# Four more pairs turned on TensorE, four more joined products, two stores at the end and a new order of the work

## The chip, the core and the metric

The kernel runs on one core of a Trainium2 chip. The metric is the device time of one execution in microseconds (us). Five engines work side by side: TensorE (PE in the profile, with its weight loads as PEld), VectorE (DVE), ScalarE (ACT), GpSimd (POOL) and the queue that issues the transfers, SyncE (SP). Each engine runs its own instructions strictly in the order in which the program lists them, and waits for the others by semaphores.

## What is computed

Two stages follow one another. The first is an attention with random features, for 8 batches of 8 heads, 576 positions of 64 numbers and 128 features. The second is a layer with a gate, applied to the 4608 tokens that come out.

```python
def phi(x):
    h = x @ omega.T - sum(x * x) / 2
    return exp(h - max(h)) / sqrt(m)
q_p, k_p = phi(q_s), phi(k_s)
kv, z = k_p^T v, sum(k_p)
out = (q_p @ kv) / (q_p @ z + 1e-06)
x = out, heads side by side: 4608 tokens of 512
h = x @ w_in
g = h * erf(softplus(h))
return g @ w_out
```

## The kernel before, in words

Two heads make a pair, and there are 32 pairs (N, line 32), numbered 0 to 31, four for each batch. For each pair TensorE projects k and q on omega, VectorE takes maxima, and ScalarE the exponentials. That gives the features `fk` and `fq`, 128 positions by 128 features in nine blocks. Then `key_values` (line 1103) sums the product of k's features with v into the bank `kvp` (36 small matmuls), and `attend` (line 1129) multiplies q's features with it into the banks `nd` (36 more; "the last product" in what follows). For `nd` q's features must lie with the features on the partitions, so `fq` has to be turned. This is done in two ways:

- For pairs below ROWS = 20 (line 785), `turn` (line 1118) has TensorE transpose the nine blocks, three into each of three PSUM banks `pt`. A copy for each bank by ScalarE or VectorE brings them into the tile `qh`.
- For pairs 20 to 31, `flip` (line 1080) transposes 32 by 32 blocks in one VectorE instruction. SyncE then stores the whole to DRAM (`dq<-fq`) and fetches it back in four transfers (`qh<-dq`), which put the blocks in their places. For these pairs the exponentials of q are written in another order of the blocks.

BEHIND (line 791) is `range(8, 31)`: for those pairs the product `nd` of a pair n is not a step of its own. It is issued right behind `kvp` of pair n + 1, as one step (`key_values` with `beside`, line 1103). For the other pairs `nd` is a step of its own. The quotients are written to the tile `y`, which serves two pairs and of which there is one (SLOTS, line 79). VectorE transposes it, and SyncE's transfers `xs<-y` bring it to the tokens' tile `xs`.

The second stage takes the tokens in six groups (SUPERS, line 33): two of 2 times 288 tokens, then four of 2 times 432. A group runs four quarters of the inner layer. Each quarter has a first product (banks `h`, `hX`, `hY`, `hZ`), the gate on ScalarE, VectorE and GpSimd, and a second product (banks `o`, `oX`, `oY`, `oZ`), which is added into the output tile `os`. Every number is held as a high and a rest part, so that each product is three matmuls. From the third group on, seven products stand for eight, with sums of blocks that VectorE and GpSimd make (tiles `xc` and `gs`). In the last quarter of a group the output rows leave: `keep` (line 1378) issues one store for both token halves `t` of a row tile, which `gemm2` (line 1413) asks for when the second half is done.

The attention of later batches runs between the products of earlier groups. The order is not written out by hand. `build` lists some 4,660 steps with a duration each, and `Plan.order` (line 154) gives each engine, one step at a time, the ready step with the earliest due time. The due times come from the plan of the second stage, carried backwards through the dependencies. The list `DATES` (line 336) then adds a correction to them, by the number of the step:

```python
        for i, x in DATES:
            ops[i].due += x
```

What comes out is the order of the instructions on every engine, SyncE's queue among them. `emit` writes them in that order, and it is fixed when the kernel runs.

Of the kernel before, what the change touches and what calls it, by code (L numbers as in the profile page):

```python
# [108 lines left out]
class Plan:  # L109
# [44 lines left out]
    def order(self, slots, caps):  # L154
# [59 lines left out]
        while True:  # L214
# [121 lines left out]
DATES = ((0, -155.4), (1, 0.9), (2, -0.7), (4, -446.6), (5, -58.8), (6, -11.2), (7, -171), (8, -17.9),  # L336
# [445 lines left out]
YFLIP = 1.5  # L782
YDMA = 4.0
ISSUE = 0.5
ROWS = 20
BOTH = 12
SUMA = ()
JOIN = 1
# [1128 lines left out]
```

## Time and profile before

| what | value |
|---|---|
| median of three runs | 978.97 us (974.37, 978.97 and 979.22) |
| the profiled execution's own time | 971.93 us |
| its span, first to last instruction | 970.2 us |
| PE busy | 954.5 us of it, 98% |
| DVE busy | 761.5 us, 78% |
| ACT busy | 625.4 us, 64% |
| POOL busy | 583.4 us, 60% |
| moved by DMA | 255.64 MB, 263 GB/s on the mean |

The profile shows one execution. Busy time of an engine counts each instant in which at least one of its instructions runs. Matmuls overlap (a matmul of 432 columns shows some 0.36 us, and the next starts 0.20 us after it), so that the rate is read from starts. Line 1523 is the helper that records all instructions; groups are told apart by their tiles.

### The profile page before, as it was taken

The numbers are of one execution on the slowest core, as the hardware profiler recorded it, in microseconds if no ns is written. First come the engines' busy times: TensorE is split into PE (matmuls) and PEld (weight loads), VectorE is DVE, ScalarE is ACT, GpSimd is POOL, SyncE is SP. The second block draws the span as 40 slices with busy tenths as digits, with TensorE's granted clock in tenths as the row PEclk, the third lists the DMA queues.
The fourth block names the chain that finished last, engine by engine and source line by source line (L and its number), as shares of the span: only waits on it lengthen the run. The fifth ranks groups of instructions, "written<-read, shape, count | busy, mean of one in ns | idle before, by whom it ended". The sixth has DMA issues, their size and how long they took to land.

```text
span 970.2 us, 20988 instructions
## 1 busy us (share of the span) xinstructions
PE 954.5 (98%) x7868; PEld 903.8 (93%) x7868; DVE 761.5 (78%) x1161; ACT 625.4 (64%) x1157; POOL 583.4 (60%) x416
## 2 busy tenths in 40 slices
PE   8999999999999999999998999999999999999998
PEld 8899999999999999999998999888999999999997
DVE  6879788767777977768797879789898699668674
ACT  7869787875866766665476375666747547564650
POOL 3234534947747666748496758388686486548620
PEclk9999999999999999999999999999999999999999
DMA  8667779598897798897898999998998776697651
GB/s 250 213 212 235 236 258 329 206 329 317 309 282 227 254 322 285 257 316 232 272 316 249 385 294 322 288 301 262 292 307 248 249 243 219 215 309 220 222 184 74
DMA packets 116388, 255.64 MB, mean 263 GB/s; under 512 B 14272, under 2 KB 31168, under 8 KB 116288
## 3 DMA queue, kind: packets, MB, share of 16 engines
q1 hardware_dynamic: 116128, 254.24, 79.9%
q8 instruction: 63, 1.03, 0.4%
q14 instruction: 37, 0.30, 0.1%
q10 hardware_dynamic: 160, 0.07, 0.0%
HBM read 194.74 MB, written 50.07 MB: 252 GB/s over the span
## 4 chain that ended last, share of the span: by engine, by line
PE 56%; DMA 4%; DVE 4%; SPq 0%; ACT 0%; issue 0%; DVEq 0%; ACTq 0%
PE hX L1523 13%; PE oX L1523 11%; PE hY L1523 7%; PE o L1523 7%; PE oY L1523 5%; PE hZ L1523 4%; PE oZ L1523 3%; DMA wb<-wdc 2%; PE kvp L1523 2%; PE nd L1523 1%; PE p0k L1523 1%; PE p1k L1523 1%; DMA y<-xN 1%; DMA xs<-y 1%; DMA wb<-wdw 1%; DVE os L1523 1%
## 5 line engine op out<-in xcount | busy, mean ns | idle before, releaser
L1523 POOL TENSOR_TENSOR hs<-gs,hs 128x864 f32<-128x864 f32 (+1 forms) x56 | 111.2, 2012 | 112.0 <-ACT gs L1523 82.8
L1523 PE MATMUL o<-gh,w 128*128 128x288 f32 (+1 forms) x704 | 167.4, 317 | 0.0
L1523 PE MATMUL hX<-xh,wb 128*128 128x432 f32 x512 | 161.6, 361 | 1.8 <-DVE y L1523 1.4
L1523 PEld LDWEIGHTS o<-gh,w 128*128 128x128 f32 x704 | 120.8, 188 | 2.1
L1523 PE MATMUL h<-xh,w 128*128 128x288 f32 x512 | 110.6, 300 | 0.0
L1523 PE MATMUL o<-gl,w 128*128 128x288 f32 (+1 forms) x352 | 110.0, 312 | 0.0
L1523 PEld LDWEIGHTS hX<-xh,wb 128*128 128x128 f32 x512 | 96.1, 188 | 7.9 <-issue 1.8
L1523 ACT ACTIVATE hs<-hX 128x432 f32<-128x432 f32 x65 | 34.7, 533 | 104.0 <-PE hX L1523 103.2
L1523 PE MATMUL oX<-th,wb 128*128 128x432 f32 x312 | 97.4, 360 | 2.2 <-DVE os L1523 2.2
L1523 PE MATMUL hX<-xl,wb 128*128 128x432 f32 x256 | 91.8, 359 | 0.0
L1523 ACT ACT_TABLE_LOAD x67 | 86.0, 1283 | 2.1 <-PEq L1908 0.7
L1523 PE MATMUL hY<-xh,wb 128*128 128x432 f32 x256 | 84.0, 363 | 1.2 <-ACT fk L1523 0.4
L1523 PEld LDWEIGHTS h<-xh,w 128*128 128x128 f32 x512 | 84.2, 188 | 0.9 <-ACT fk L1523 0.2
L1523 PE MATMUL h<-xl,w 128*128 128x288 f32 x256 | 75.4, 295 | 0.0
L1523 DVE TENSOR_TENSOR os<-oX,os 128x432 f32<-128x432 f32 x86 | 50.9, 600 | 24.5 <-PE oX L1523 24.3
L1523 ACT ACTIVATE gs<-hs 128x1728 f32<-128x1728 f32 (+1 forms) x48 | 69.4, 1483 | 0.4
L1523 ACT ACTIVATE gs<-gs 128x1728 f32<-128x1728 f32 (+1 forms) x48 | 69.1, 1480 | 0.3
L1523 PEld LDWEIGHTS o<-gl,w 128*128 128x128 f32 x352 | 66.3, 188 | 0.9
L1523 PEld LDWEIGHTS oX<-th,wb 128*128 128x128 f32 x312 | 58.6, 188 | 5.9 <-DVE os L1523 2.9
L1523 POOL TENSOR_TENSOR bl<-hs,bh 128x864 fp32r<-128x864 f32 x22 | 57.5, 2634 | 0.0
L1523 PE MATMUL oX<-tl,wb 128*128 128x432 f32 x156 | 55.9, 359 | 0.0
L1523 POOL TENSOR_TENSOR tl<-gs,th 128x864 fp32r<-128x864 f32 x20 | 44.5, 2246 | 18.8 <-ACT th L1523 13.9
(162 smaller groups left out, 2699.9 us busy)
## 6 DMA issues: line engine op xcount, KB each, us to landing
wb<-wdc SPq DMA_DIRECT2D x232, 256.0 KB, 4.6
wb<-wdw SPq DMA_DIRECT2D x174, 256.0 KB, 4.8
w<-wdw SPq DMA_DIRECT2D x44, 512.0 KB, 6.1
st<-w SPq DMA_DIRECT2D x32, 512.0 KB, 5.7
wdw<-w SPq DMA_DIRECT2D x32, 512.0 KB, 4.7
wdc<-c SPq DMA_DIRECT2D x32, 512.0 KB, 5.9
x<-xR SPq DMA_DIRECT2D x20, 576.0 KB, 6.5
y<-xN SPq DMA_DIRECT2D x20, 576.0 KB, 6.3
```

Source lines behind the costliest of these rows:

```text
L1523: return tc.keep_in_program_order(method(*args, **kwargs))
```

## The change

Four things are changed together:

- ROWS goes from 20 to 24: pairs 20 to 23 take `turn` in place of `flip`, and their q keeps the plain layout and the plain order of the exponentials.
- BEHIND goes from `range(8, 31)` to `range(4, 31)`: `nd` of pairs 4 to 7 is issued behind `kvp` of pairs 5 to 8.
- In the last group `keep` is called for each token half: eight stores of one half in place of four of both.
- DATES is another list, with 2,281 corrections where there were 2,992, so that the whole order of the steps is new.

```diff
-DATES = ((0, -155.4), (1, 0.9), (2, -0.7), (4, -446.6), (5, -58.8), (6, -11.2), (7, -171), (8, -17.9),
...
+DATES = ((0, -150.3), (4, -232.6), (5, 4.5), (6, -14.6), (7, -138.9), (13, -28.1), (14, 2.5),
...
-ROWS = 20
+ROWS = 24
...
-BEHIND = range(8, 31)
+BEHIND = range(4, 31)
...
-    def keep(b, et, o):
-        pl.op("ostore", [("S", 0.1, 1e9)], lambda e: E.o_store(o, b, et), reads=[(o, 0), (o, 1)],
-              plan=clock[0] + 3.0, size=P * 2 * SUPERS[b][0] * 4)
+    def keep(b, et, o, ts=(0, 1)):
+        pl.op("ostore", [("S", 0.1, 1e9)], lambda e: E.o_store(o, b, et, ts), reads=[(o, t) for t in ts],
+              plan=clock[0] + 3.0, size=P * len(ts) * SUPERS[b][0] * 4)
...
                 out(t)
-                if q == NQ - 1 and t:
+                if q == NQ - 1 and b == len(SUPERS) - 1:
+                    keep(b, et, o, (t,))
+                elif q == NQ - 1 and t:
                     keep(b, et, o)
...
-        def o_store(self, o, b, et):
-            sp.dma_start(out[et][:, FROM[b]:FROM[b + 1]], o.ap.rearrange("p t c -> p (t c)"))
+        def o_store(self, o, b, et, ts):
+            T = SUPERS[b][0]
+            at, n = FROM[b] + ts[0] * T, len(ts) * T
+            sp.dma_start(out[et][:, at:at + n], o.ap[:, ts[0]:ts[-1] + 1].rearrange("p t c -> p (t c)"))
```

## Rows read from the trace of the kernel before

**Rows 1.** The page's first part: busy us, share of the span, instructions of each engine.

```profile
PE 954.5 (98%) x7868; PEld 903.8 (93%) x7868; DVE 761.5 (78%) x1161; ACT 625.4 (64%) x1157; POOL 583.4 (60%) x416
```

**Rows 2.** Busy time by stretch: stretch, its length, engines, granted clock, DMA share, GB/s.

```profile
60.00:450.00 390.00, 389.45 (x3633) 376.09 (x3632) 304.87 (x516) 280.84 (x564) 232.87 (x191) 1.00 0.82 275
450.00:580.00 130.00, 127.34 (x1105) 117.94 (x1103) 105.92 (x158) 77.69 (x159) 88.32 (x62) 1.00 0.91 296
580.00:780.00 200.00, 196.30 (x1498) 181.44 (x1497) 168.38 (x233) 123.77 (x208) 140.98 (x84) 1.00 0.88 282
```

**Rows 3.** PE's waits, whole span: us in total, times, the longest.

```profile
PE oX L1523 <- DVE os L1523: 2.2, 2, 1.2
PE hX L1523 <- DVE y L1523: 1.4, 1, 1.4
PE pt L1523 <- ACT fq L1523: 1.1, 2, 0.6
```

**Rows 4.** Groups of instructions by form: count, busy us, mean ns, idle before.

```profile
L1523 PE MATMUL pt<-ident,fq 128*128 128x128 f32 x180 | 27.1, 277 | 1.1 <-ACT fq L1523 1.1
...
L1523 ACT ACTIVATE qh<-pt 128x384 f32<-128x384 f32 x39 | 18.7, 492 | 24.1 <-PE pt L1523 23.8
...
L1523 DVE STREAM_TRANSPOSE fq<-fq 128x1152 f32<-128x1152 f32 x12 | 16.4, 1367 | 0.1
...
L1523 DVE COPY qh<-pt 128x384 f32<-128x384 f32 x21 | 11.0, 550 | 1.7 <-PE pt L1523 1.4
```

**Rows 5.** PE in order of time around three transposes: start, us, instruction.

```profile
443.77 0.49 PE L1523 MATMUL pt<-ident,fq 128*128 128x128 f32 x3
444.01 0.44 PE L1523 MATMUL o<-gh,w 128*128 128x432 f32 x1
444.29 0.36 PE L1523 MATMUL o<-gl,w 128*128 128x432 f32 x1
```

**Rows 6.** PE in order of time: nd alone, kvp alone, then both joined.

```profile
100.46 0.30 PE L1523 MATMUL o<-gh,w 128*128 128x288 f32 x1
100.69 1.27 PE L1523 MATMUL nd<-kh,qh 128*64 128x65 f32 x36
...
106.09 1.37 PE L1523 MATMUL kvp<-v,fk 128*64 128x130 f32 x36
107.39 0.40 PE L1523 MATMUL o<-gh,w 128*128 128x288 f32 x1
...
417.84 1.37 PE L1523 MATMUL kvp<-v,fk 128*64 128x130 f32 x36
419.04 1.22 PE L1523 MATMUL nd<-kh,qh 128*64 128x65 f32 x36
```

**Rows 7.** The longest chain from 522 to 542 us: start, us, what.

```profile
527.96 2.78 DMA xs<-y
...
531.01 0.83 DVE y L1523 x2
```

**Rows 8.** SyncE's queue and VectorE in order of time, the same stretch.

```profile
513.79 3.98 SPq L1523 DMA_DIRECT2D qh<-dq  x4
...
531.01 0.82 DVE L1523 TENSOR_TENSOR y<-nd,rc 128x320 f32<-128x320 f32 x2 [3.90 <-DMA wb<-wdw]
```

**Rows 9.** DMA issues of the round trip: count, KB each, median us to landing.

```profile
dq<-fq SPq DMA_DIRECT2D x12, 576.0 KB, 6.1
qh<-dq SPq DMA_DIRECT2D x48, 144.0 KB, 5.6
```

**Rows 10.** The end: the chain from 955 us on, then two stretches as in Rows 2.

```profile
954.91 11.04 PE o L1523 x56
...
965.97 0.61 DVE os L1523
...
967.50:968.00 0.50, 0.00 (x0) 0.00 (x0) 0.00 (x0) 0.00 (x0) 0.00 (x0) 1.00 1.04 429
968.00:968.50 0.50, 0.00 (x0) 0.00 (x0) 0.00 (x0) 0.00 (x0) 0.00 (x0) 1.00 0.94 387
```

775 rows, old and new, of the table DATES are left out of this document.

## The prediction, made before the change was run

> **What bounds the kernel.** I began with the page's first part: PE is busy for 954.5 of 970.2 us [rows 1]. Whoever wants to shorten this kernel can take work from PE, or one of the 15.7 us in which PE does nothing, and there is little else. DVE, ACT and POOL are far from full. The next view is busy time by stretch, which tells where those 15.7 us lie. From 60 to 450 us PE is idle for 0.55 us in 390. From 450 to 580 it is idle for 2.66 us, and from 580 to 780 for 3.70 us [rows 2]. The last matmul ends at 965.95 us (954.91 + 11.04) [rows 10], so that 4.25 us of the span lie behind it. What is left, 15.7 - 0.55 - 2.66 - 3.70 - 4.25 = 4.5 us, lies at the start, where the first pairs are worked alone. [...]
>
> The third view is PE's waits. The longest are for sums into the output tile and for the tile y, both on DVE [rows 3]. For the largest stall the chain from 522 us on names the cause: a transfer from y to xs begins at 527.96 us and lands 2.78 us later. Only then, at 531.01 us, can DVE write the next quotients into y [rows 7]. DVE had stood still for 3.90 us before them [rows 8]. (The row blames a transfer of weights; the chain and the kernel, which has one tile y, say that it was the reading of y.) DVE's sums for PE stand behind those quotients in its queue, and PE waits 1.4 us and then 1.2 us [rows 3], which is all of the 2.66 us. The transfers from y were themselves late in SyncE's queue. Before them stand the four fetches of a flipped pair, which hold the queue for 3.98 us [rows 8].
>
> **The change, part by part.** *Turning pairs 20 to 23 on PE.* Three transposes and the matmul behind them take 444.29 - 443.77 = 0.52 us; a plain matmul is 0.197, so that the three cost 0.32 us [rows 5, 10]. With nine to a pair and four pairs that is 12 times 0.32 = 3.9 us, all of it on the engine that sets the end. It can't be less, since PE has no idle time there to hide it in. The upper bound is the duration of one transpose taken alone, 277 ns [rows 4], times 36: 10.0 us. I take 3.9, because twenty pairs before it are turned and their rows overlap in this way.
>
> [...]
>
> *What the turning adds elsewhere.* Twelve copies from PSUM, each 492 ns on ACT or 550 ns on DVE; in the share of the earlier ones (39 to 21), eight on ACT and four on DVE [rows 4]: 3.9 and 2.2 us. ACT is busy for 77.7 of 130 us there [rows 2] and can take them. If it were held by other work when PE needs the copy, PE would wait; that is a rival below.
>
> *What the flipping took.* Four transposes of 1.37 us on DVE [rows 4], 5.5 us. With the copies DVE is left with 3.3 us less. From SyncE's queue go four stores and sixteen fetches; at 3.98 us for four fetches [rows 8] that is 16 us of the queue. From the DMA engines go four times 576 KB out and the same back [rows 9], 4.7 MB. This stretch moves 296 GB/s at a share of 0.91 [rows 2], so that they are worth 16 us of it. None of this is PE's work, and it counts only where it ends a stall. It can end one: pair 22's four fetches are those that stood ahead of the transfers from y. Some 4 us less in that queue is more than the 3.90 us for which DVE stood still. So I take the whole stall, 2.7 us, as gone. The bounds are 0, if something else in the queue takes their place, and 2.7. What is late next is then DVE alone, with its sums for the blocks; it keeps its work after 540 us.
>
> *The joined products, pairs 4 to 7.* A product nd on its own starts 0.23 us after the matmul before it starts [rows 6]; a matmul of 288 columns takes two thirds of 0.197, so that 0.10 us go for the entry. A kvp on its own takes 1.30 us until the next, and with nd behind it 1.20 us [rows 6]. One join thus saves 0.2 us at least, and twice that at most, if the matmul behind also starts slower. I take the middle, 0.3: four joins give 1.2 us (0.8 to 1.6). The join moves nd later, by as much as the next pair's kvp is later. The work that hides this is the second stage's, since the tokens of that group are wanted only much later. If that cover were gone, PE would wait at the second group's start.
>
> *The last store in two.* Behind the last sum (965.97 + 0.61) the store moves its 432 KB in about 1 us, nearly all of it between 967.5 and 968.5 [rows 10]. The first half is 12 matmuls, 2.4 us, older, and leaves before. The last half is 0.5 us shorter. Bounds: 0, if only the way there and back counts, and 1.0. Three further stores are earlier and end nothing. Their issues come when the queue has little else.
>
> *The new order.* No row shows it. It moves the instructions on every engine and every transfer in SyncE's queue. What it can gain at most is what is left of the stalls: 0.55 and 3.70 in the middle, and some 3 of the 4.5 at the start, 7.2 us in all. What it can lose is bounded by the same rows: the stalls of both stretches over again, 6.4 us. I take a gain of 2.0, nearer to nothing than to the best, because DVE loses 3.3 us of work and SyncE 16, which leaves an order more room, though ahead of 540 us and not where most of these stalls lie.
>
> **The sum** is +3.9 - 1.2 - 0.5 - 2.7 - 2.0 = -2.5 us. Against the profiled execution's own 971.93 us that is 969.4. This execution was 7 us faster than the median of the three runs shown, 978.97, and the runs spread over 4.9. I carry the difference over to the median: 976.5 us, 0.3% less.
>
> **The rivals.** *A: the order ends nearly all stalls.* To gain more than 0.5% (4.9 us) the three counted parts, +3.9 - 1.2 - 0.5 = +2.2, need 7.1 of the 9.9 us of stalls (2.7 and 7.2) to go. With all of them gone it is -7.7, or 971.3. For it: with turning alone, from 60 to 450 us, the same kernel loses 0.55 us [rows 2]. Against it: the stalls after 580 us are DVE's, and only pairs that still flip stand there.
>
> *B, slower: the copies come too late.* Each turn needs three PSUM banks, which fall free only when the copies have run, and nd waits for all three copies. Where ACT is late a turn waits, as two did, for 1.1 us together [rows 3]. At 0.55 us for each of twelve, with the old stall still there, it is +2.2 + 6.6 = +8.8, or 987.8. It decides from 2.7 us of new waiting on, five of the twelve. For it: the four pairs lie where the seven products want the same banks. Against it: pairs up to 19 did it at a cost of 0.55 us.
>
> *C: the stall only moves, and the order gains nothing.* +2.2, or 981.2. SyncE's queue is long, and another transfer may stand ahead of y's.
>
> *D: transposes that do not overlap*, each started by a late exponential, at 277 ns [rows 4]: 10.0 in place of 3.9, +3.6, or 982.6. The rows of the turn speak against it. [...]
>
> **How the numbers follow.** A change of 0.5%, 4.9 us, is about what a measurement of this kernel can tell from none: 974.1 to 983.9 is the same. My forecast has a chance of 0.35, C 0.15 and D 0.03, all three within it. A has 0.28 and B 0.19, with any order that makes as much new waiting. That is 0.28 faster, 0.53 the same, 0.19 slower. The range takes in A and, below it, the runs' own spread, to 967. Above, it takes in C and D and ends at 984, where B begins.
>
> **What the profile after would show.** There should be 216 transposes into pt, 8 of fq on DVE, 8 stores dq and 32 fetches. PE's idle time between 450 and 580 us should be under 1 us, with no chain through xs<-y there. The last transfer should end 0.5 us sooner behind the last sum. Nd should stand alone for pairs 0 to 3 and the last only. The forecast is wrong if PE's busy time grows by much more than 3 us, if PE waits for qh or pt appear in the middle, or if idle time between 60 and 780 us is above 9 us or below 1.

## The result, and the profile after

The changed kernel takes 989.15 us (985.82 to 992.39, five runs) where the kernel before takes 978.97 on the same chip: 1.0108 times the time, with an interval of 1.0074 to 1.0143. It is slower by 1.1%, and the forecast of 976.5 us, with its range of 967 to 984, was wrong. The profiled execution took 985.85 us, its span 984.0.

The page's first part answers to [rows 1]:

```profile
PE 960.0 (98%) x7904; PEld 909.6 (92%) x7904; DVE 760.1 (77%) x1134; ACT 638.2 (65%) x1182; POOL 581.0 (59%) x427
```

PE has 36 instructions more, the transposes, and is busy for 5.5 us more (a part of that, an estimated 1.8 us, is a lower clock, told below). It is idle for 984.0 - 960.0 = 24.0 us, where it was 15.7. So 8.3 of the 13.8 us are idle time. The view by stretch tells where, with the columns of [rows 2]:

```profile
60.00:450.00 390.00, 385.81 (x3619) 373.01 (x3618) 296.35 (x498) 279.28 (x550) 231.94 (x199) 1.00 0.81 273
450.00:580.00 130.00, 129.56 (x1077) 120.03 (x1076) 102.68 (x151) 92.71 (x183) 95.18 (x60) 1.00 0.78 255
580.00:780.00 200.00, 191.57 (x1494) 177.57 (x1493) 166.42 (x218) 117.27 (x214) 130.99 (x91) 0.98 0.87 274
```

From 450 to 580 us PE is idle for 0.44 us: the old stall is gone. But there are 4.19 us from 60 to 450, where there was 0.55, and 8.43 from 580 to 780, where there were 3.70. The first 60 us have 6.66 us, where there were 4.52. PE's waits (us in total, times, the longest) are led by two that are not in [rows 3]:

```profile
PE hY L1422 <- DVE os L1422: 5.2, 1, 5.2
PE hY L1422 <- ACT fk L1422: 3.2, 1, 3.2
PE nd L1422 <- DVE qh L1422: 2.5, 2, 2.1
PE h L1422 <- ACT kh L1422: 1.6, 1, 1.6
PE pt L1422 <- ACT qh L1422: 1.4, 1, 1.4
```

The first two are 8.4 us, and both are told in the order of time on VectorE and GpSimd. The first:

```profile
631.03 0.42 DVE L1422 TENSOR_REDUCE pm<-pm 128x2 f32<-128x256 f32 x1
631.36 8.10 DVE L1422 TENSOR_TENSOR tl<-gs,th 128x1728 fp32r<-128x1728 f32 x1
631.47 4.02 POOL L1422 TENSOR_TENSOR bl<-hs,bh 128x864 fp32r<-128x864 f32 x2
635.44 2.21 POOL L1422 TENSOR_TENSOR gs<-hs,gs 128x432 f32<-128x432 f32 x2
639.39 0.68 DVE L1422 TENSOR_REDUCE pm<-p0k 128x4 f32<-128x512 f32 x1
...
644.07 0.47 PE L1422 MATMUL hY<-xh,wb 128*128 128x432 f32 x1 [3.23 <-ACT fk L1422]
```

(The helper that records all instructions is line 1422 here, 1381 or 1382 in the experiments.) VectorE's `tl<-gs,th`, which takes 1.9 to 3.8 us elsewhere, lasts 8.10 us. GpSimd meanwhile runs four instructions without a break, the last of which ends at 635.44 + 2.21 = 637.65, and `tl` ends 1.81 us after that. Four reductions and two small instructions, the last of which makes `mx`, stand behind it in VectorE's queue; ScalarE's `fk` waits for `mx`, and PE waits for the banks that `fk` empties. The second:

```profile
673.03 1.16 POOL L1422 TENSOR_TENSOR xc<-xs,xs 128x432 f32<-128x432 f32 x1
...
674.03 6.76 DVE L1422 TENSOR_TENSOR xc<-xs,xs 128x432 f32<-128x432 f32 x1
674.11 4.11 POOL L1422 TENSOR_TENSOR hs<-gs,hs 128x864 f32<-128x864 f32 x2
678.17 2.16 POOL L1422 TENSOR_TENSOR gs<-hs 128x432 f32<-128x432 f32 x2
...
681.52 0.60 DVE L1422 TENSOR_TENSOR os<-oX,os 128x432 f32<-128x432 f32 x1
```

A sum `xc` of this size takes 0.60 us at 681.00 and 6.76 here, and ends 0.46 us behind GpSimd's last of four (678.17 + 2.16 = 680.33). The sum `os` stands behind it, and PE waits 5.2 us for its bank. There is a price on top. In the stretch after that gap the granted clock is 0.69. From 682 to 686 us it is 0.50, and eleven times the next matmul of 432 columns starts 0.36 us after the one before it (682.70 to 686.66). From 690 to 692 it is 1.00, and there they start 0.20 us apart. Eleven times 0.16 is an estimated 1.8 us:

```profile
682.00:690.00 8.00, 7.82 (x88) 7.09 (x89) 5.15 (x7) 7.10 (x21) 1.64 (x1) 0.69 0.04 6
```

The counted parts did what the text said. The groups answer to [rows 4], and the chain's end to [rows 10]:

```profile
L1422 PE MATMUL pt<-ident,fq 128*128 128x128 f32 x216 | 33.6, 277 | 1.9 <-ACT qh L1422 1.4 <-ACT fq L1422 0.4
...
L1422 DVE STREAM_TRANSPOSE fq<-fq 128x1152 f32<-128x1152 f32 x8 | 10.9, 1366 | 0.0
```

```profile
965.93 14.37 PE o L1422 x73
980.31 0.02 issue
980.33 0.61 DVE os L1422
```

There are 216 transposes and 8 flips. Behind the last matmul (980.30) lie 3.7 us, where there were 4.25: 0.55 us less.

### The profile page after: what moved, and what is told of

It reads as the page before. It is cut to its first block, busy times and chain, and to the rows that moved or that the text cites. A ratio compares the mean times of both kernels' runs of the same rounds, so it can differ in the third digit from the quotient of the medians.

```text
span 984.0 us, 21048 instructions
## 1 busy us (share of the span) xinstructions
PE 960.0 (98%) x7904; PEld 909.6 (92%) x7904; DVE 760.1 (77%) x1134; ACT 638.2 (65%) x1182; POOL 581.0 (59%) x427
## 4 chain that ended last, share of the span: by engine, by line
PE 86%; DVE 5%; DMA 5%; issue 1%; ACT 1%; SPq 1%; POOL 0%; DVEq 0%; ACTq 0%
PE o L1422 16%; PE hX L1422 13%; PE oX L1422 12%; PE h L1422 10%; PE hY L1422 7%; PE oY L1422 6%; PE hZ L1422 4%; PE kvp L1422 3%; PE nd L1422 3%; PE oZ L1422 3%; PE pt L1422 2%; PE p0k L1422 2%; DMA st<-w 2%; DMA uq<-qT 2%; PE p1k L1422 1%
## 5 line engine op out<-in xcount | busy, mean ns | idle before, releaser
L1422 PE MATMUL hX<-xh,wb 128*128 128x432 f32 x512 | 164.0, 363 | 0.4 <-DVE hs L1422 0.4
L1422 POOL TENSOR_TENSOR hs<-gs,hs 128x864 f32<-128x864 f32 (+1 forms) x46 | 93.2, 2050 | 102.6 <-ACT gs L1422 102.5
L1422 ACT ACTIVATE hs<-hX 128x432 f32<-128x432 f32 x78 | 41.4, 532 | 110.4 <-PE hX L1422 109.2
L1422 PEld LDWEIGHTS hY<-xh,wb 128*128 128x128 f32 x256 | 48.6, 190 | 11.5 <-DVE os L1422 5.6
L1422 POOL TENSOR_TENSOR tl<-gs,th 128x864 fp32r<-128x864 f32 x24 | 52.6, 2219 | 10.5 <-ACT th L1422 7.4
L1422 POOL TENSOR_TENSOR y<-y 128x288 f32<-128x288 f32 x42 | 36.8, 902 | 36.9 <-issue 16.3
```

The lines of the kernel that those rows point to most:

```text
L1422: return tc.keep_in_program_order(method(*args, **kwargs))
```

## The experiments

Theory: **the new order made the loss, and mostly by two VectorE instructions that start while GpSimd works through a list of its own and end only behind it (8.10 and 6.76 us above).** Rivals: the counted parts cost more than their rows said; the stalls were an accident of one execution. To move one instruction and nothing else, these kernels take the steps from a written-out list in place of the planner's choice:

```diff
-    for o in plan.order(slots, CAPS):
+    for item in ORDER:
```

**E1, two places mended.** The changed kernel; only VectorE's order differs.

```diff
 pm<-pm
-tl<-gs,th
 pm<-p0k
...
 hs<-hX,hs
 th<-gs
+tl<-gs,th
...
 pm<-p1q
-xc<-xs,xs
 pm<-s,pm
 mx<-s,pm
-xc<-xs,xc
 os<-oX,os
-xc<-xs,xc
 hs<-hX
+xc<-xs,xs
+xc<-xs,xc
+xc<-xs,xc
```

> The changed kernel, with two places of VectorE's order altered and nothing else: tl<-gs,th (631.36 us) goes behind the reductions that follow it, and three instructions of xc (674.03 us) behind the sum os and the copy hs that follow them. Theory (the new order made the loss, and it made it by having these two instructions ask for SBUF while GpSimd works through its list): PE's waits of 3.2 us at 644 and of 5.2 us at 682 go, with up to 2 us of lower clock behind them, so that PE's idle time from 580 to 780 us falls from 8.4 to 2 to 4 us and the time to 978 to 982 us (ratio to the kernel before 0.999 to 1.004). Rival (the counted parts cost more than their rows said): the two stalls may go, but PE waits again a little later for the same sums, and the time stays at 986 to 990 us (1.007 to 1.011).

Measured: 982.16 us, 1.0058 times before (1.0032 to 1.0083), where the changed kernel in the same company (E4) took 989.83. Two places of one queue are worth 7.7 us. PE's idle time from 580 to 780 us fell to 3.86:

```profile
580.00:780.00 200.00, 196.14 (x1554) 181.04 (x1554) 163.23 (x227) 123.31 (x223) 131.19 (x92) 1.00 0.91 284
...
PE hZ L1382 <- DVE hs L1382: 2.2, 1, 2.2
PE h L1382 <- ACT kh L1382: 1.9, 1, 1.9
```

The two waits are gone, and the clock is 1.00. A new wait of 2.2 us for `hs` took the place of part of them, at 684 us, so that the gain stops just short of the range expected.

**E4, the changed kernel again.** No edit: a second profiled execution.

> The changed kernel once more, for a second profiled execution of it. Theory (the stalls lie in the order and not in one execution): PE stops at the same two instructions, near 644 and 682 us, for 2 to 4 and 4 to 6 us, with tl<-gs,th and xc<-xs,xs on VectorE at 6 us or more; 986 to 992 us. Rival (they were an accident of the profiled execution): PE's stalls of over 1 us lie at other instructions.

Measured: 989.83 us, 1.0132 (1.0106 to 1.0157). The same two instructions, and longer:

```profile
632.14 9.18 DVE L1382 TENSOR_TENSOR tl<-gs,th 128x1728 fp32r<-128x1728 f32 x1
...
677.45 7.23 DVE L1382 TENSOR_TENSOR xc<-xs,xs 128x432 f32<-128x432 f32 x1
```

PE waited 4.3 and 5.7 us behind them. The stalls belong to the order, not to one execution.

**E11, one place earlier.** Is it the moment of asking, or GpSimd's unbroken list?

```diff
+tl<-gs,th
 pm<-pm
-tl<-gs,th
...
+xc<-xs,xs
 pm<-p1q
-xc<-xs,xs
```

> The changed kernel with the two instructions tl<-gs,th and xc<-xs,xs each one place earlier on VectorE (ahead of the reduction pm<-pm at 631.0, and of pm<-p1q at 673.4 us), so that they ask for SBUF 0.4 and 0.7 us sooner, while GpSimd is in the same instruction. Theory (VectorE is kept out for as long as GpSimd's instructions follow one another without a break, whenever it asks): both take 7 us or more again, and the time is 986 to 991 us (ratio to the kernel before 1.010 to 1.015). Rival (it is the moment of asking: VectorE goes in at the next boundary, as at nearly all others): both take under 4.5 us, PE's stalls at 644 and 682 us shrink by 4 us or more together, and the time is 980 to 985 us.

Measured: 989.2 us, 1.0164 (1.0116 to 1.0212). Both were held again, for 8 us and more:

```profile
630.30 8.87 DVE L1382 TENSOR_TENSOR tl<-gs,th 128x1728 fp32r<-128x1728 f32 x1
631.17 4.03 POOL L1382 TENSOR_TENSOR bl<-hs,bh 128x864 fp32r<-128x864 f32 x2
635.17 2.20 POOL L1382 TENSOR_TENSOR gs<-hs,gs 128x432 f32<-128x432 f32 x2
...
675.23 8.11 DVE L1382 TENSOR_TENSOR xc<-xs,xs 128x432 f32<-128x432 f32 x1
```

GpSimd ended at 637.37 and `tl` 1.80 us later, the same 1.8 as in the changed kernel. Starting sooner did not end it sooner: its end kept that distance from the end of GpSimd's list.

**E2, the order alone.** The new order with the other parts undone. The flips of pairs 20 to 23 stand where their first turns stood, the fetches some 6 us behind.

```diff
-ROWS = 24
+ROWS = 20
-BEHIND = range(4, 31)
+BEHIND = range(8, 31)
-                if q == NQ - 1 and b == len(SUPERS) - 1:
+                if False:
```

> The new order with the other three parts undone (20 pairs turned, products joined from pair 8, one last store of both halves). Theory (the order is the cause): PE's busy time falls by some 2.7 us, but most of the new idle time stays, 20 us or more in all, and the time is 983 to 990 us (ratio to the kernel before 1.005 to 1.011). Rival (the parts are the cause): 970 to 979 us (0.992 to 1.000), with 16 us idle or less.

Measured: 1006.05 us, 1.0296 (1.0265 to 1.0327), beyond either theory. Both stalls are there again (PE waits of 3.8 and 5.8 us), so they do not come from the parts. But the largest wait is another:

```profile
PE nd L1381 <- DMA qh<-dq: 12.6, 3, 6.6
```

This order leaves no time for the round trip through DRAM that it no longer has to make, so that the run says less of the order's own price than was meant.

**E3, turning alone**, in the order of before but for some places (told under E10).

```diff
-ROWS = 20
+ROWS = 24
```

> The order of before, with pairs 20 to 23 turned on TensorE and nothing else of the change. Theory (the part costs what its rows said): PE busy for 3 to 5 us more, the stall at 529 to 533 us gone (2.7 us less idle), 979 to 982 us (ratio 1.000 to 1.004). Rival (copies come too late, or the transposes do not overlap): PE waits at pt or qh for 4 us or more from 450 to 580 us, 985 us or more (1.007 or more).

Measured: 980.13 us, 1.0033 (1.0009 to 1.0057). The stretch of the old stall has no idle time at all:

```profile
450.00:580.00 130.00, 130.00 (x1104) 120.26 (x1103) 107.79 (x157) 79.44 (x173) 90.34 (x62) 1.00 0.79 255
580.00:780.00 200.00, 194.56 (x1522) 178.77 (x1519) 162.35 (x234) 124.99 (x211) 139.06 (x82) 1.00 0.90 284
```

PE is busy for 961.3 us, 3.4 more than in E9 (the kernel before again, below), and the stall of some 3 us is gone, as priced; no copy of the four turned pairs came too late. PE's longest wait for a copy, 4.5 us, stands before the first `nd` at 18.9 us, far from the change; E9 has 1.7 there and the changed kernel 2.1 and 3.2. Matmul for matmul, this execution is already 3.3 us behind E9 at 60 us, before any turned pair, and 3.4 us at the end. From 580 to 780 us 5.44 us are idle (E9: 4.67), with a wait for `os` at 710 us that the order of before does not show.

**E9, the kernel before again.**

> The kernel before once more, for a second profiled execution of it: the first took 971.93 us where the median is 976.6. Theory (the first was a fortunate one, and the stalls at the start and at 700 to 715 us which every kernel in its order has shown since belong to the order): about 976 us, with 2 to 4 us more idle time of PE in the first 60 us or a stall of 1.5 to 2.5 us near 710 us (oY waiting for os). Rival (these stalls come from the changes made): the idle time lies as in the first execution, within 1 us in each stretch, whatever the total.

Measured, in one execution: 976.92 us.

```profile
0.00:60.00 60.00, 55.28 (x683) 51.15 (x684) 44.77 (x101) 44.14 (x138) 23.20 (x28) 0.97 0.76 211
450.00:580.00 130.00, 126.94 (x1096) 117.58 (x1095) 102.93 (x155) 76.31 (x163) 85.72 (x62) 0.99 0.90 289
580.00:780.00 200.00, 195.33 (x1490) 179.82 (x1489) 170.09 (x234) 126.82 (x210) 138.23 (x82) 1.00 0.90 283
```

The rival held: the same stalls in the same stretches, 3.06 and 4.67 us against 2.66 and 3.70, and 4.72 at the start against 4.52, each within 1 us of the first execution. There is no wait at 710 us. Of the 5 us more, 3.4 are PE's busy time (957.9 us against 954.5, the same matmuls), with a granted clock of 0.97 in the first 60 us. PE's counts are compared with this execution from here on.

**E5, joins and the last store alone**, in the order of before but for some places (told under E10); the quotients and transfers behind the moved products are moved with them.

```diff
-BEHIND = range(8, 31)
+BEHIND = range(4, 31)
...
+                if q == NQ - 1 and b == len(SUPERS) - 1:
+                    keep(b, et, o, (t,))
```

> The order of before with the joined products of pairs 4 to 7 and the last output in two stores, without the four turned pairs. Theory (the parts cost what their rows said): four joins give 0.8 to 1.6 us and the store 0.5, so that the time falls by 1.3 to 2.1 us (ratio to the kernel before 0.997 to 1.000), and the stall at 529 to 533 us stays. Rival (the joined product holds its banks longer, and the pairs in the first 120 us are the ones with no other work beside them): PE gets new waits for a bank at nd, kvp or h before 120 us, and the time rises by 2 us or more (1.002 or more).

Measured: 982.98 us, 1.0064 (1.0039 to 1.0088): a loss of 6.3 us where a gain was priced. ScalarE tells of one cause:

```profile
61.96 1.16 ACT L1382 ACTIVATE uk<-uk 64x1152 f32<-64x1152 f32 x1 [2.00 <-DMA uk<-kT]
63.02 0.26 ACT L1382 ACTIVATE kh<-kvp 128x130 f32<-128x130 f32 x1
...
63.34 0.40 PE L1382 MATMUL h<-xh,w 128*128 128x288 f32 x1 [1.53 <-ACT kh L1382]
```

A joined step ends one product later, and so the copy `kh` that empties the bank `kvp` got its place in ScalarE's queue behind `uk`, which stands waiting for a transfer. The changed kernel has the same at 62 us (its 1.6 us above).

**E10, that one mended**: `kh` ahead of `uk`, the rest as in E5.

```diff
-uk<-uk
 kh<-kvp
+uk<-uk
```

> The joined products and the two stores in the old order again (e5), with kh of pair 5 ahead of uk on ScalarE, where e5 showed PE waiting 1.5 us at 63.3. Theory (the join itself is worth what its rows said, 0.3 each, and what it cost came from the one instruction that fell behind a waiting one): the stall goes, 979.5 to 981.5 us (ratio to the kernel before 1.003 to 1.005). Rival (the rest of the loss, too, hangs on the first stall): 976 to 978 us (0.999 to 1.002). Second rival (the wait moves on): 982 us or more.

Measured: 981.97 us, 1.007 (1.0043 to 1.0098). The wait is gone and the time is the same, so that the last rival comes nearest. The longest wait that is left:

```profile
PE oY L1382 <- DVE os L1382: 4.9, 3, 2.2
```

The joins themselves did what they were priced at. Up to pair 9's product kvp PE spent 23.22 us on kvp and nd, counted from each start to the next, where E9 spent 24.43 on the same matmuls: 1.2 us for four. In the same stretch the products `h`, `ppq` and `pt` took 2.9 us more, in short waits. The wait of 2.2 us is again the one at 710 us.

What makes that wait can be read in VectorE's queue, in E9 first and then in E3:

```profile
706.70 0.61 DVE L1381 TENSOR_TENSOR os<-oY,os 128x432 f32<-128x432 f32 x1 [0.57 <-PE oY L1381]
708.40 1.34 DVE L1381 TENSOR_REDUCE s<-y 128x18 f32<-128x1152 f32 x1
...
708.33 1.35 DVE L1381 TENSOR_REDUCE s<-y 128x18 f32<-128x1152 f32 x1 [1.51 <-POOL y L1381]
709.60 0.60 DVE L1381 TENSOR_TENSOR os<-oY,os 128x432 f32<-128x432 f32 x1
710.25 0.46 PE L1381 MATMUL oY<-bh,wb 128*128 128x432 f32 x1 [1.72 <-DVE os L1381]
```

In the order of before the reduction `s<-y` stands behind three sums into `os`. In E3, E5, E6 and E10 it stands ahead of them and waits for GpSimd, and PE waits for the sums: 1.7, 2.5, 2.1 and 2.2 us. Pairs 4 to 7 and 20 to 23 are long done there. So the lists of these four runs are not the order of before with the parts alone: in E3 some 28 VectorE instructions other than turns, flips and copies stand in other places. The times of E3, E5, E6 and E10 are those of the parts and of such moves together. No run has the parts without them.

**E6, all three parts in the order of before** (the edits of E3 and E5, with the same reservation).

> All three counted parts in the order of before: pairs 20 to 23 turned, pairs 4 to 7 joined, last output in two stores. Theory (the parts add up): the measured +3.3 of the turning alone less 1.3 to 2.1, 977.7 to 978.5 us where before is 976.5 (ratio 1.001 to 1.003), some 4 us under the changed kernel with its two places mended. Rival (the parts need the new order to fit): 982 us or more (1.006 or more).

Measured: 983.57 us, 1.0072 (1.0046 to 1.0098). The parts do not add up there as priced; but they cost 6 us less than in the new order.

**E7, five places mended** in the changed kernel: E1 and three more.

```diff
-uk<-uk
 kh<-kvp
+uk<-uk
...
-gh<-hs
 qh<-pt
+gh<-hs
...
-xh<-xc
 hs<-hZ,hs
+xh<-xc
```

> The changed kernel with the two places of e1 and three more: on ScalarE kh (62.3 us) goes ahead of uk, which stood waiting for a transfer, and qh (225.3 us) between the two halves of gh; on VectorE hs<-hZ (683.5 us) goes ahead of xh. Theory (what is left of the loss is again single instructions that stand behind a waiting or long one): 1.9 + 1.5 + 2.2 us of PE's idle time go, 976 to 978 us (ratio to the kernel before 0.999 to 1.002). Rival (the order is short everywhere and a mended place only moves the wait on): 980 us or more (1.004 or more).

Measured: 979.95 us, 1.0028 (1.0007 to 1.0049). The waits at 62 and 226 us went: 1.90 us are idle from 60 to 450, where E1 has 4.50. The third stayed, at 2.8 us, and for the old reason:

```profile
671.57 4.08 POOL L1382 TENSOR_TENSOR hs<-gs,hs 128x864 f32<-128x864 f32 x2
671.96 6.29 DVE L1382 TENSOR_TENSOR xc<-xs,xs 128x432 f32<-128x432 f32 x1
...
680.00:690.00 10.00, 7.85 (x21) 6.72 (x22) 9.39 (x11) 2.44 (x7) 8.38 (x6) 0.53 0.45 151
```

The last line is the stretch behind the wait: its granted clock is 0.53. In E1 GpSimd's list began 2 us behind the same `xc` (677.82 against 675.75), which took 1.15 us.

**E8, the old order mended.** If an order can lose so much in single places, that of before might gain in its own. With the last store in two:

```diff
 SyncE
-wb<-wdc (two)
 xs<-y (eight)
-wb<-wdc (two)
 xs<-y (one)
+wb<-wdc (four)
 VectorE
+os<-oX,os
 pm<-p1k
 pm<-p1q
-os<-oX,os
...
-xl<-xc,xh
 os<-oY,os
 os<-oX,os
+xl<-xc,xh
```

> The kernel before with the last output in two stores and its own three largest stalls mended: on SyncE four fetches of weights go behind the last transfer xs<-y (527.96 us); on VectorE the sum os (608.64 us) goes ahead of two reductions, and xl<-xc,xh (659.51 us) behind the two sums that follow it. Theory (a stall is the instruction or transfer that stands ahead, and moving that ends it): 2.6 + 1.0 + 0.6 us of PE's idle time go and 0.5 at the end, 970.9 to 973.5 us where before is 976.5 (ratio 0.994 to 0.997). Rival (the wait moves on to the next block): no change, 975.5 to 977.5 us.

Measured: 976.23 us, 0.9989 (0.9969 to 1.0009): no change. The stall at 532 us is gone, and this stands in its place:

```profile
569.27 2.04 SPq L1381 DMA_DIRECT2D qh<-dq  x4
...
575.48 0.81 PE L1381 MATMUL nd<-kh,qh 128*64 128x65 f32 x10 [2.91 <-DMA qh<-dq]
```

**E12, the fetches earlier.** As E8 without the move of `xl`, and with those four fetches ahead of two of `wb` and five of `xs`.

```diff
+qh<-dq (four)
 wb<-wdw (two)
 xs<-y (five)
-qh<-dq (four)
```

> The old order mended as in e8, with xl<-xc,xh left at its old place (e8 showed a new wait of 2.4 us at 673 behind it) and the four fetches qh<-dq that PE waited for at 575 us in e8 issued ahead of two fetches of weights and five transfers xs<-y (561 us), 4 us sooner. Theory (in e8 the stall at 532 us was gone and its 2.6 us came back where a fetch was then late): neither stall is there, PE's idle time from 450 to 580 us is under 0.5 us, and the time is 972.5 to 974.5 us where before is 976.3 (ratio 0.996 to 0.998). Rival (the stretch is bound by the transfers as a whole, and another one comes late): 1.5 us or more of PE's waits for a transfer remain from 530 to 600 us, and the time is 975.5 to 978 us.

Measured: 977.43 us, 1.0002 (0.9983 to 1.0021). From 450 to 580 us 1.28 us are idle. But the next wait lies just behind:

```profile
450.00:580.00 130.00, 128.72 (x1115) 118.99 (x1115) 105.39 (x155) 74.91 (x158) 84.47 (x61) 1.00 0.88 286
540.00:560.00 20.00, 20.00 (x178) 18.62 (x178) 17.88 (x24) 10.06 (x28) 17.09 (x11) 1.00 1.04 391
...
PE p1k L1381 <- DVE y L1381: 1.5, 1, 1.5
```

From 540 to 560 us the DMA share is 1.04 (1.04 in E9 too), so that the transfers there may have no room for a PE that comes sooner. That this makes the wait at 582 us is not shown: VectorE had stood 3.2 us for a tile `y` of GpSimd's just before it. No version was found that beats the kernel before.

## Why the prediction was wrong, point by point

- **The new order: wrong, and it made most of the loss.** The step said: "I take a gain of 2.0", bounded by 7.2 us of stalls that could go and by "the stalls of both stretches over again, 6.4". Measured are 989.83 - 976.52 = +13.3 us (10.2 in the result's own runs). Moving two instructions of that order took 7.7 of them back (E4 to E1), and moving three more 2.2, by the medians (E1 to E7): 9.9 us in five places, more than the bound allowed for the whole order. How the rest divides between the order and the parts is open, since E6, with a loss of 6.9 us, has an order of its own. The flaw is in the bound: stalls that an order shows say what another can save, not what it can lose. What it can lose is set by what one badly placed instruction holds up. A row for that was in the trace of before: a `tl<-gs,th` that took 4.96 us while GpSimd ran three instructions, with nobody waiting behind it:

```profile
597.15 4.96 DVE L1523 TENSOR_TENSOR tl<-gs,th 128x1728 fp32r<-128x1728 f32 x1
598.11 2.19 POOL L1523 TENSOR_TENSOR gs<-hs,gs 128x432 f32<-128x432 f32 x2
```

- **The turning on PE: right.** 3.9 us of busy time were taken (with 0.197 us for a plain matmul, 11.04 us over 56 [rows 10]), 3.4 measured (E3 against E9); counted from starts, as the prediction did, E3's twelve groups come to 4.0. The transposes overlap: in E3 0.245 us pass from the start of three of them to the start of the matmul behind, less than the 277 ns that one of them lasts [rows 4]. Rivals B and D fell: no wait for copies of pairs 20 to 23 appeared. The changed kernel did wait 1.4 us for a copy of an earlier pair, at 224 us; in E7 it is 0.3.
- **The old stall: gone as said, its worth not.** 0.44 us are idle in its stretch, in E3 0.00. But the kernel with the turning alone is 3.2 us slower (1.0033), not 1.2, though the interval (0.9 to 5.6) holds both. What the turning costs by itself stays open: 1.7 us of waiting at 710 us are not its own, and in the two profiled executions 3.3 of the 3.4 us between E3 and E9 lie ahead of any turned pair. E8 and E12 show that 2.7 us saved at this stall need not arrive: another transfer is late next, or VectorE's quotients further on. Rival C had this for the stall's own place; it happened one block later.
- **The joined products: the size right, the cover wrong.** 1.2 us were taken, 1.2 measured on PE itself (E10 against E9). (A matmul of 288 columns, put at two thirds of 0.197 us, has 0.13 in the trace of before: six starts in a row, from 99.80 to 100.46 us, lie 0.13 apart.) "The work that hides this is the second stage's" failed: it isn't `nd` that comes late, but what queues behind the longer step, first `kh`. Where all of E5's 6.3 us come from stays open: `kh` explains none of it in the end (E10), and the wait of 2.5 us at 710 us comes from a place of the order far behind the joins.
- **The last store: right.** 0.5 us were taken and 0.55 measured.
- **The side and the chances.** Slower had 0.19, for late copies "with any order that makes as much new waiting". It was the second, and the text had given it no mechanism. The prediction's own test, idle time above 9 us between 60 and 780, was met: 4.19 + 0.44 + 8.43 = 13.06. Its test on PE's busy time tells less: that grew by 5.5 us, but E9 shows 3.4 us more with no change at all.

What remains after five mends is 3.4 us (979.95 against 976.63). E3 lost about as much, but that does not make it the cause: E7's trace still has the wait of 2.8 us and, behind it, a clock of 0.53 from 680 to 690 us.

## What to carry to other kernels

A change that comes with a new order of everything isn't priced by its parts: here PE's work for each part was priced to half a microsecond, and two instructions in one queue cost 7.7 us. Before a new order is believed, look in its trace for instructions that last three times their usual time, and at what stands behind them in their queue; E1 gained by putting `tl` and `xc`, which had lasted 8.10 and 6.76 us while GpSimd ran four instructions without a break, behind the small ones that others wait for. When one part is to be tried alone in an old order, compare every engine's order with the old one first: in E3, E5, E6 and E10 one reduction that stood elsewhere made PE wait some 2 us. And a stall that is mended can come back at the next block, as in E8 and E12: count it as gained only when the end comes sooner.

## What the runs showed of the hardware

A VectorE instruction can be held through several GpSimd instructions in a row, and not only through one. In the changed kernel's trace `tl<-gs,th` takes 1.94 us on VectorE at the least, and up to 8.10 where it began within an instruction of GpSimd. Not every kind is held: the 158 sums of 432 columns into `os` that read a bank (`oX`, `oY` or `oZ`) took 0.61 us at most, the 92 among them too that began within an instruction of GpSimd. What the two engines share no run shows; that it is SBUF, as two expectations have it, was the author's reading. A wait for one instruction of GpSimd, some 2 us here, would not give these times: the waits were 6.2 us (8.10 less 1.94, and 6.76 less 0.60) for four instructions of GpSimd that followed at once, and 6.6 to 7.5 us in E4 and E11.

Mostly the wait ends with one. In the fourteen profiled executions 964 VectorE instructions lasted at least 0.3 us longer than the quickest tenth of their kind and size, began within an instruction of GpSimd, and GpSimd's next came within 0.1 us of that one's end. 941 of them ended within their own undisturbed length behind that first change, 23 did not, and of these 9 waited through three or more further ones. All nine are the `tl` at 630 to 648 us and the `xc` at 672 to 693. Each of them ended at one and the same distance behind the end of GpSimd's list, 1.81 to 1.82 us for `tl` and 0.46 to 0.47 for `xc`, 0.13 to 0.14 us less than its own undisturbed length. What tells them from the others is open. It is not the moment of the start, which lay from 0.14 us (E4) to 1.7 us (E7) ahead of the change; and it came every time that the two started ahead of that list of GpSimd's or, in E7, within its first instruction (the changed kernel twice, E2 and E11, and E7 for `xc`).
